# Eleven idle matmuls between the last transposes of q' and the first k^T v of batch 0

## The chip, the cores and the metric

The kernel runs on one core of a Trainium2 chip. The metric is the device time of one execution in microseconds (us). A core has five engines with queues of their own: TensorE (PE, with its weight loads as PEld), VectorE (DVE), ScalarE (ACT), GpSimd (POOL) and SyncE (SP). They wait for each other by semaphores. Each engine takes its instructions in the order in which the program lists them.

## The reference

Linear attention with cosine weights, and a feed-forward layer on its output. The shapes are 8 batches, 8 heads, 576 positions and a head dimension of 64; the layer has d_model 512 and d_ff 2048, on 4608 rows.

```python
def phi(x, c, s):                       # c = cos(pi/2 * pos/S), s = sin(pi/2 * pos/S)
    r = np.maximum(x, 0.0)
    return np.concatenate([r * c, r * s], axis=-1)
q_p, k_p = phi(q, c, s), phi(k, c, s)   # 64 -> 128 columns
kv  = np.einsum('bhsf,bhsd->bhfd', k_p, v)
z   = np.sum(k_p, axis=2)
num = np.einsum('bhsf,bhfd->bhsd', q_p, kv)
den = np.einsum('bhsf,bhf->bhs', q_p, z)[..., None] + 1e-06
x   = (num / den), as rows of (batch, position) by 512
h = x @ w_in
out = (h * sigmoid(1.702 * h)) @ w_out
```

## The kernel before

All of it runs in bf16 with sums in f32. The rows of x are cut into nine blocks of 512. A block's first layer is `mm1` (line 281: four matmuls of 128x512 for each of 16 slices of d_ff, then a gelu on ACT, line 286), its second is `mm2` (line 321: 16 matmuls of 128x512 for each of four row tiles). In the main loop from line 476 the attention of batch i + 1 is laid between the matmuls of block i, at steps written out by hand. The order on every engine is the order of the program text: the schedule is manual.

Before that loop stands a start of its own for batch 0, lines 356 to 473; the change lies in it. It runs as follows.

- `warmup(12)` (line 422) issues twelve matmuls of 128x512 on a tile of zeros, `warm`; nothing reads their result. They stand in PE's queue while q of batch 0 is on its way.
- For four quarters (n, p) of q, the half of the heads n and the pair of row chunks p, `prep_q0` makes q' = relu(q) times cosine and sine (line 207 on DVE, line 205 on ACT), and `turn_q0` turns it: eight transposes on PE (line 364) into one bank of the tile `mm`, and one copy on ACT to `qT` (line 365). After each quarter but the last, `warmup(2)` adds two idle matmuls.
- `prep(0, "k", ...)` makes k' the same way, twelve calls: for the first half of the heads chunks 0 to 5, and then for the second half. All cosines are on DVE; of the sines, those of chunks 3 to 5 are on ACT (line 205), the others on DVE.
- `kv0` (line 373) is k^T v and the sum of k' in one: for each head six matmuls, one for each chunk, with 128 columns (v and a column of ones, stepped over). `kv_lo` has heads 0 to 3, `kv_hi` heads 4 to 7 in two calls; ACT casts each part to `kvs` (line 375).
- `num0` (line 382) makes numerators and denominators for half of the heads and two row chunks, eight matmuls with 65 columns. `den0` and `product0` divide on DVE (lines 392 to 401), `turn_x0` turns the result on PE (line 409) and ACT copies it to `xT` (line 411).
- `mm1_first` (line 417) makes the first four slices of the first layer for block 0 in parts, as the pieces of `xT` come.

PSUM tiles come from two rings: `mm`, four buffers of one bank each, and `at`, two buffers of two banks each. A tile's first writer waits until the readers of the buffer's last tile are done. In the start `mm` serves the four `turn_q0`, then `kv_lo`, `kv_hi` and the four accumulators of `mm1_first`, in this order. The idle matmuls of `warmup` take an `at` tile.

k of batch 0 is loaded by POOL's queue in two halves and v in three parts (line 86), behind q, which SP's queue loads (line 120).

Of the kernel before, what the change touches and what calls it, by code (L numbers as in the profile page):

```python
# [21 lines left out]
def kernel(  # L22
# [9 lines left out]
    nc = tc.nc  # L32
# [21 lines left out]
    def rows(c):  # L54
        return 128 if c < 4 else 64

    def wide(b, n):
        return b < 2 and n != "q"

    def krows(b, c):  # L60
        return 96 if b < 2 else rows(c)

    warm = const.tile([128, TB], BF16)
    nc.vector.memset(warm, 0.0)

    def mm_tile():
        return ps.tile([128, TB], F32, name="mm", bufs=4)

    def at_tile():
        return ps.tile([128, 2, 512], F32, name="at", bufs=2)  # L70

    def warmup(n):
        wps = at_tile()
        for _ in range(n):
            nc.tensor.matmul(wps[:, 0], warm[:, 0:128], warm, start=True, stop=True)


    state = {b: {} for b in range(B)}
# [103 lines left out]
    def part(b, n, c, h0, h1):  # L182
        if wide(b, n):
            return state[b][n][:96, 0:48 * D].rearrange("p (h c d) -> p c h d", c=6, d=D)[:, c, h0:h1]
        if c == 4:
            return state[b][n, 4].rearrange("p (h d) -> p h d", d=D)[:, h0:h1]
        return state[b][n][:, 0:32 * D].rearrange("p (h c d) -> p c h d", c=4, d=D)[:, c, h0:h1]
# [7 lines left out]
    def qn_slot(b, c):  # L195

        return state[b]["qn4"] if b < 2 and c == 4 else state[b]["qn"][:rows(c), c]

    def prep(b, n, c, h0=0, h1=H, on=(nc.vector, nc.vector)):
        r = rows(c) if n == "q" else krows(b, c)  # L200
        for cs, w in enumerate((cos6, sin6) if wide(b, n) else (cosw, sinw)):
            o = qn_slot(b, c) if n == "q" else kp[:r, c]
            oc, i, wc = o[:, h0:h1, cs * D:cs * D + D], part(b, n, c, h0, h1), w[:r, c:c + 1]
            if on[cs] is nc.scalar:
                nc.scalar.activation(oc, i, AF.Relu, scale=wc)  # L205
            else:
                nc.vector.tensor_scalar(oc, i, 0.0, wc, op0=MAX, op1=MUL)  # L207
# [159 lines left out]
    def kv0(kv, h0, h1):  # L367

        v3 = s0["v"][:96].rearrange("p (j d) -> p j d", d=D)
        for h in range(h0, h1):  # L370
            for c in range(6):
                j = h * 6 + c
                nc.tensor.matmul(kv[:, ts(h % 4, 128)].rearrange("p (j d) -> p j d", j=2), kp[:96, c, h, :],  # L373
                                 v3[:, j:49:48 - j, :], start=(c == 0), stop=(c == 5))
        nc.scalar.copy(s0["kvs"][:, h0 // 4, h0 % 4:h0 % 4 + h1 - h0, 0:D + 1],
                       kv.rearrange("p (h e) -> p h e", e=128)[:, h0 % 4:h0 % 4 + h1 - h0, 0:D + 1])
# [43 lines left out]
    AC, VE = nc.scalar, nc.vector  # L420
    kvs_new(0)
    warmup(12)

    def prep_q0(n, p, on=(VE, VE)):
# [5 lines left out]
    for n, p in ((0, 0), (0, 1), (1, 0), (1, 1)):  # L430
        if n:
            prep_q0(n, p)
        turn_q0(n, p, AC.copy)
        if (n, p) != (1, 1):
            warmup(2)
    for n in range(2):
        for c in range(6):
            prep(0, "k", c, 4 * n, 4 * n + 4, on=(VE, AC if c > 2 else VE))
    kv_lo, kv_hi = mm_tile(), mm_tile()
    kv0(kv_lo, 0, 4)  # L440
    kv0(kv_hi, 4, 6)
# [122 lines left out]
```

## Time and profile before

| | |
|---|---|
| median of 4 runs | 300.36 us |
| the runs | 298.69, 300.30, 300.42, 302.07 us |
| the profiled execution | 298.91 us |
| its span, first to last instruction | 296.9 us |
| PE busy in the span | 284.2 us (96%) |
| mean granted clock of PE | 0.991 |
| `warmup` (line 75) matmuls | 18, 379/492/634 ns (least, median, most) |
| k^T v (line 373) matmuls | 48, of 219 ns in the median |

The profile is of one execution. Times in it are in us from the first instruction, and "idle before" a group is the time that its engine stood still ahead of it, with what ended the wait. Matmuls are pipelined: one of 219 ns is followed by the next after a quarter of that, so the distance between starts tells more than the duration. The granted clock is that of PE, as a share of the full one.

### The profile page before, as it was taken

What the parts mean: (1) busy time and instruction counts of PE and PEld (TensorE: products, weight loads), DVE (VectorE), ACT (ScalarE), POOL (GpSimd) and SP (SyncE); (2) the same over time, 40 slices, a digit from 0 to 9 for tenths busy, and PEclk for the clock granted to TensorE, in tenths of its full rate; (3) what the DMA queues carried; (4) which work ended last, traced back from release to release, by engine and by line L of the source; (5) the groups of instructions that cost most, each with busy time, mean ns of one, the idle gap of its engine ahead of it and who ended that gap; (6) DMA issues with size and microseconds to landing.
All of it is one profiled execution on the core that took longest, in us unless ns stands there. A gap on an engine that the chain in (4) does not pass through costs nothing.

```text
span 296.9 us, 5089 instructions
## 1 busy us (share of the span) xinstructions
PE 284.2 (96%) x1940; PEld 146.9 (49%) x1974; DVE 105.7 (36%) x357; ACT 126.0 (42%) x215; POOL 94.8 (32%) x117
## 2 busy tenths in 40 slices
PE   8778999999999999999999999999999999999994
PEld 3575456545444554455445544554455444444443
DVE  5751454683490158115811482148214200000000
ACT  6836623663127412651175116511751166127411
POOL 8542330540259025800690159004401200120021
PEclk9979999999999999999999999999999999999998
DMA  8999999599999977995799879965902510011033
GB/s 195 186 204 199 203 198 191 154 127 173 155 208 170 185 121 137 183 193 100 137 179 174 124 138 194 186 104 116 194 3 60 121 42 1 35 71 38 0 71 71
DMA packets 87303, 39.65 MB, mean 134 GB/s; under 512 B 57136, under 2 KB 85040, under 8 KB 87280
## 3 DMA queue, kind: packets, MB, share of 16 engines
q0 software_dynamic: 40848, 27.01, 58.6%
q1 hardware_dynamic: 46272, 12.20, 24.4%
q8 instruction: 15, 0.25, 0.3%
q10 hardware_dynamic: 160, 0.13, 0.2%
q14 instruction: 8, 0.07, 0.1%
HBM read 36.70 MB, written 9.44 MB: 155 GB/s over the span
## 4 chain that ended last, share of the span: by engine, by line
PE 87%; DMA 5%; DVE 3%; ACT 3%; issue 1%; ACTq 0%; DVEq 0%
PE mm L281 39%; PE mm L321 37%; DMA qT<-qn 4%; PE at L265 3%; PE at L244 3%; PE mm L417 2%; DMA q<-in_q_dram 1%; DVE qn L207 1%; PE mm L345 1%; ACT g L286 1%; PE mm L373 1%; DVE xb L273 1%; ACT qT L226 1%; ACT kp L205 0%; PE mm L364 0%
## 5 line engine op out<-in xcount | busy, mean ns | idle before, releaser
L321 PE MATMUL mm<-w_out_sb,g 128*128 128x512 bf16 x543 | 126.4, 379 | 0.6
L281 PE MATMUL mm<-xT,w_in_sb 128*128 128x512 bf16 x547 | 122.7, 377 | 0.9
L333 POOL DMA_DIRECT2D out_dram<-ysb x54 | 50.6, 941 | 174.4 <-ACT ysb L331 172.9
L286 ACT ACTIVATE g<-mm 128x512 bf16<-128x512 f32 x144 | 85.6, 598 | 45.9 <-PE mm L281 44.9
L281 PEld LDWEIGHTS <-w_in_sb 128*128 128x128 bf16 x564 | 54.4, 98 | 64.1 <-issue 0.2
L321 PEld LDWEIGHTS <-g 128*128 128x128 bf16 x560 | 52.1, 98 | 57.0
L331 ACT COPY ysb<-mm 128x512 f32<-128x512 f32 x34 | 19.9, 585 | 98.3 <-PE mm L321 94.9
L248 DVE CAST kvs<-at 128x260 bf16<-128x260 f32 x14 | 5.4, 426 | 60.5 <-PE at L244 60.5
L273 DVE TENSOR_TENSOR xb<-at,inv 128x512 bf16<-128x512 f32 (+1 forms) x36 | 24.8, 689 | 1.2
L271 DVE TENSOR_SCALAR den<-at 128x8 f32<-128x8 f32 (+1 forms) x36 | 5.9, 164 | 44.4 <-PE at L265 44.4
L350 DVE COPY ysb<-mm 128x256 f32<-128x256 f32 x1 | 0.4, 424 | 59.4 <-PE mm L345 59.4
L265 PEld LDWEIGHTS <-qT 128*128 128x128 bf16 x272 | 12.9, 98 | 8.8 <-DMA qT<-qn 0.9
L207 DVE TENSOR_SCALAR qn<-q,cosw 128x512 bf16<-128x512 bf16 (+1 forms) x36 | 12.7, 356 | 11.4 <-DMA q<-in_q_dram 11.4
L265 PE MATMUL at<-kvs,qT 128*128 128x65 bf16 x272 | 14.2, 194 | 1.0 <-DMA qT<-qn 0.4
L207 DVE TENSOR_SCALAR qn<-q,sinw 128x512 bf16<-128x512 bf16 (+1 forms) x34 | 13.0, 381 | 0.0
L86 POOL DMA_DIRECT2D v<-in_v_dram x10 | 9.3, 943 | 5.3 <-DMA w_in_sb<-in_moe_w_in_dram 2.7
L244 PEld LDWEIGHTS <-kp 128*128 128x128 bf16 (+1 forms) x288 | 9.6, 97 | 1.6
L244 PE MATMUL at<-vt,kp 128*128 128x65 bf16 (+1 forms) x288 | 9.8, 193 | 0.0
L86 POOL DMA_DIRECT2D k<-in_k_dram x9 | 7.8, 865 | 4.1 <-DMA q<-in_q_dram 3.3
L207 DVE TENSOR_SCALAR kp<-k,cosw 128x512 bf16<-128x512 bf16 x24 | 8.3, 348 | 0.0
L207 DVE TENSOR_SCALAR kp<-k,sinw 128x512 bf16<-128x512 bf16 x24 | 8.1, 336 | 0.0
L272 DVE RECIPROCAL inv<-den 128x8 f32<-128x8 f32 (+1 forms) x36 | 7.2, 201 | 1.2
(75 smaller groups left out, 136.2 us busy)
## 6 DMA issues: line engine op xcount, KB each, us to landing
out_dram<-ysb POOLq DMA_DIRECT2D x38, 128.0 KB, 2.9
out_dram<-ysb POOLq DMA_DIRECT2D x16, 256.0 KB, 2.7
q<-in_q_dram POOLq DMA_DIRECT2D x7, 512.0 KB, 9.2
k<-in_k_dram POOLq DMA_DIRECT2D x6, 512.0 KB, 10.7
v<-in_v_dram POOLq DMA_DIRECT2D x6, 512.0 KB, 12.2
w_out_sb<-in_moe_w_out_dram POOLq DMA_DIRECT2D x4, 512.0 KB, 18.3
w_in_sb<-in_moe_w_in_dram POOLq DMA_DIRECT2D x3, 512.0 KB, 12.1
q<-in_q_dram SPq DMA_DIRECT2D x2, 512.0 KB, 4.3
```

What stands on the lines that cost most here:

```text
L86: on.dma_start(out=state[b][n][:np_, t * D * h0:t * D * h1].rearrange("p (h e) -> p h e", h=h1 - h0), in_=SRC[n][b, h0:h1, 0:np_ * t, :].r ...
L207: nc.vector.tensor_scalar(oc, i, 0.0, wc, op0=MAX, op1=MUL)
L244: nc.tensor.matmul(kv[:, ds(h % 4 * (D + 1), D + 1)], kp[:r, c, h, :], vt[:r, c, h, 0:D + 1], start=(c == 0), stop=(c == last))
L265: nc.tensor.matmul(nm[:, h // 4, ds(h % 4 * (D + 1), D + 1)], q_slot(b, c)[:, h, :], state[b]["kvs"][:, h // 4, h % 4, 0:D + 1], start=Tru ...
L272: nc.vector.reciprocal(inv[:r], den[:r])
L273: nc.vector.tensor_tensor(state[b]["xb"][:r, c].rearrange("p (n h) d -> p n h d", n=2), nm4[:, :, :, 0:D], inv[:r].unsqueeze(3).to_broadca ...
L281: nc.tensor.matmul(hps[:, c0:c1], w_in_sb[:, kc, ds(fc * 128, 128)], xT[:, kc, ds(i * TB + c0, c1 - c0)], start=(kc == 0), stop=(kc == KC ...
L286: nc.scalar.activation(g, hps, AF.Gelu_apprx_sigmoid)
L321: nc.tensor.matmul(yps, gT[fc][:, ds(t * 128, 128)], w_out_sb[:, fc, :], start=(fc == 0), stop=(fc == FC - 1))
L331: nc.scalar.copy(ysb, cur[t])
L333: nc.gpsimd.dma_start(out=out[row:row + (n - 1) * step + 1:step, :], in_=ysb[p0:p0 + n, :])
L417: nc.tensor.matmul(first[fc][:, c0:c1], w_in_sb[:, kc, ts(fc, 128)], xT[:, kc, c0:c1], start=(kc == 0), stop=(kc == KC - 1))
```

## The change

One call of `warmup` is added, between the making of k' and `kv0`, so on PE it stands behind the last eight transposes of q' and ahead of the first matmul of k^T v. It issues eleven matmuls of 128x512 on the tile of zeros. They write a tile of their own from the ring `mm`, so that the tiles taken after it each move on by one buffer in this ring. For that, `warmup` gets a second argument, the tile to write to; without it, it takes an `at` tile as before.

```diff
-    def warmup(n):
-        wps = at_tile()
+    def warmup(n, wps=None):
+        wps = at_tile()[:, 0] if wps is None else wps
         for _ in range(n):
-            nc.tensor.matmul(wps[:, 0], warm[:, 0:128], warm, start=True, stop=True)
+            nc.tensor.matmul(wps, warm[:, 0:128], warm, start=True, stop=True)
...
     for n in range(2):
         for c in range(6):
             prep(0, "k", c, 4 * n, 4 * n + 4, on=(VE, AC if c > 2 else VE))
+    warmup(11, mm_tile())
     kv_lo, kv_hi = mm_tile(), mm_tile()
     kv0(kv_lo, 0, 4)
     kv0(kv_hi, 4, 6)
```

## The prediction

> **What bounds the kernel now.** I read the page first (shares, slices, clock), then PE's waits, the chain over the first 26 us, PE's instructions around the change, and last load and clock in stretches of one length. The page, busy time of PE and two rows of the 40 slices:
>
> ```profile
> PE 284.2 (96%) x1940; PEld 146.9 (49%) x1974; DVE 105.7 (36%) x357; ACT 126.0 (42%) x215; POOL 94.8 (32%) x117
> ...
> PE   8778999999999999999999999999999999999994
> ...
> PEclk9979999999999999999999999999999999999998
> ```
>
> PE bounds the kernel. It stands still mainly in the first four slices (7.42 us each), and in the third its granted clock is not full. Its waits over the run, longest first:
>
> ```profile
> PE mm L373 <- DMA v<-in_v_dram: 1.7, 1, 1.7
> PE at L409 <- DVE xb L401: 1.4, 1, 1.4
> ```
>
> The first is the place of the change. The chain there (start, us, what):
>
> ```profile
> 9.27 0.63 PE mm L364 x8
> 9.90 0.02 issue
> 9.93 0.02 ACT qT L365
> 9.95 0.89 issue
> 10.84 1.31 ACT kp L205 x3
> 12.15 0.05 issue
> 12.20 1.92 PE mm L373 x31
> ```
>
> k^T v (L373) does not follow from PE's work. ACT first evicts the turned q', then makes the sine half of k' for chunks 3 to 5, and the sixth matmul starts at 12.20, when ACT has the third. The first five ran earlier, as PE's own list of instructions shows (start, us, line, tiles, count):
>
> ```profile
> 8.68 0.59 PE L75 MATMUL at<-warm 128*128 128x512 bf16 x2
> 9.11 0.78 PE L364 MATMUL mm<-ident,qn 128*128 128x128 bf16 x8
> 11.59 2.51 PE L373 MATMUL mm<-v,kp 96*128 96x128 bf16 x36 [1.70 <-DMA v<-in_v_dram]
> ```
>
> The clock is seen in stretches of 3.41 us, set where its record changes (stretch, us, PE busy with instructions, the same of PEld, DVE, ACT and POOL, clock, DMA):
>
> ```profile
> 8.43:11.84 3.41, 1.71 (x22) 1.11 (x20) 3.41 (x18) 3.19 (x6) 1.57 (x3) 1.00 1.29 198
> 11.84:15.25 3.41, 3.17 (x57) 2.93 (x55) 1.75 (x8) 2.14 (x6) 2.93 (x4) 1.00 1.17 184
> 15.25:18.66 3.41, 1.58 (x30) 1.28 (x28) 1.82 (x8) 1.40 (x4) 0.89 (x2) 1.00 1.24 207
> 18.67:22.07 3.40, 3.40 (x39) 3.40 (x37) 1.40 (x5) 0.65 (x2) 1.64 (x3) 0.50 1.39 199
> ```
>
> The clock is half in one stretch only, 18.67 to 22.07, right after a stretch of low load. The stretch with the hole that the change fills has low load too, and cost no clock in this execution.
>
> **The change part by part.** *The added matmuls.* The last transpose takes 0.219, so it starts at 9.11 + 0.78 - 0.22 = 9.67; the next instruction can start 0.06 later, at 9.73 (after the group before it: 8.62 to 8.68). Two warm matmuls fill 8.68 to 9.11, 0.215 each; eleven fill 2.37 and end at 12.10. Of these, 9.73 to 11.59 is a hole, free. Then five k^T v matmuls that ran from 11.59 on now run from 12.10: 5 x 0.056 = 0.28 (31 in 1.92 with the drain of the last), and the sixth starts at 12.38 instead of 12.20: **+0.18**. Behind it on PE lie the rest of k^T v, then the numerators (L382); for k^T v waits ACT's cast of kvs (13.46), for the numerators DVE's denominator (14.39). ACT is done with k' at 13.34, so it does not hide the delay, and from 12.20 to 25.4 the chain runs without slack. Behind that PE's waits are under 0.5 us together, on work that PE's own progress released. So the 0.18 reaches the end.
> Bounds: had k' been ready when v landed, all of 11.59 to 12.10 would be exposed, 0.5, and 0.6 with a wake-up; were ACT 0.2 later, nothing. I take 0.18, what these rows give.
>
> *The bank.* The idle matmuls write the mm bank that the first turned q' left; ACT's copy of it ended before 8.69 (two copies from 6.71 in 1.98), so they wait for nothing. All later mm tiles move one bank on: k^T v takes the banks of the second and third copies (done by 10.94 at the latest), the first of the four accumulators the fourth's bank, long free at 18.0. Cost nothing, covered by at least 1 us each; without cover, one copy of about 1 us. The changed signature of the helper costs nothing. No DMA, no queue of SP or POOL, no wait on ACT or DVE is touched.
>
> *The clock.* In the profiled execution the sum is 298.91 + 0.18 = 299.1 (298.91 is its own time: span 296.9 and 2.0 around it). But that execution lies 1.45 below the median of the runs, 300.36, so it is not the typical one, and what can differ is where the clock's stretches fall. I count the columns that PE streamed in a stretch, against 3.41 / 0.215 x 512 = 8120 at full clock. 8.43 to 11.84: 2 x 512, about 12 transposes and 5 k^T v of 128 each = 3200, 0.39; the clock stayed. 15.25 to 18.66: 14 numerators of 65, 6 transposes and 7 first matmuls of 128 = 2570, 0.32; it fell. So it falls from somewhere between 0.32 and 0.39. Now slide the first stretch 0.6 later, 9.03 to 12.44: 8 transposes, some 10 k^T v, the rest of a warm one, 2500, 0.31: below the stretch that fell. At 1.4 later (9.84 to 13.25) 24 k^T v give 3070, 0.38 again. So in about a third of all placements, 0.2 to 1.3 later, the hole should cost a half-clock stretch over k^T v: 3.41/2 = **1.7**. With the eleven matmuls (5632 columns more) every such stretch is over 0.8, so that loss goes. The later hole, before L409, stays; by the same count it costs its 1.7 in the placements that it did, and some others.
> The run times speak for such steps: 298.69, 300.30, 300.42, 302.07 and the profile's 298.91 are about 1.6 apart.
>
> Here stands a rule against the change. The Trainium skill ("TensorE: Matmul & The Clock Gate", "Part 1: The HAM clock gate") has the clock halved after an idle window of about 3.4 us, and its closing table warns of PE idle for more than about 3 us. By it the hole of 1.70 costs no clock, and the change is worth +0.18 on every run: 300.36 + 0.18 = 300.5. Against it stands the stretch at 15.25: its longest hole is 1.44, and the clock was half after it. I go by the row. The same section says that the window runs free of the kernel's start; one execution can't show that, but my slide rests on it.
>
> **The forecast and the rivals.**
> 1. *The forecast.* A typical run loses one half-clock stretch too many to this hole and is rid of it: 300.36 - 1.7 + 0.18 = 298.8 by the stretch, 299.1 by the profiled execution, which had no such loss. I take **299.1**, nearest to a row. Chance 0.50.
> 2. *The hole costs no clock in any run*, and the 1.6 steps come from transfers or from the start. For it: the hole's own stretch kept its clock here. Then 300.5, to 301.0 at the upper bound of the delay. Chance 0.28.
> 3. *Both holes lose their cost.* Where k^T v runs at half clock, all that follows comes 1.7 later, and the second hole can fall into a bad stretch because of that. Then a run that had two loses both: 300.36 - 3.4 + 0.2 = 297.2, and for a median with some runs left at one, 297.4. Against it: the second hole cost its stretch here without the first. Chance 0.14.
> 4. *Slower: the idle matmuls run at half clock themselves.* At the start the warm ones went 0.427 apart (12 from 1.20 to 5.83 with the change of pace in them). If the clock is still or again half at 9.73, eleven take 4.70, k^T v starts at 14.43, and the sixth at 14.71: +2.5, 302.9. It decides from a start of 12.10 on: each 0.1 of pace adds 1.1. Against it: the stretches before 9.73 are loaded (PE 3.02 busy in 5.01 to 8.42). Chance 0.08.
>
> **How the numbers follow.** Likeliest: 299.1. The range takes in cases 1 and 2 with the delay's upper bound (301.0) and reaches case 3's 297.4 below; case 4 and the edges are left out. About 1% (3 us) is what a measurement of this kernel can tell from no change. Faster by more than that (under 297.36) needs all of case 3 and a little more: 0.07. Slower (over 303.36) needs case 4 and k^T v slow besides: 0.03. All else, 0.90, is within.
>
> **What the changed profile would show.** Eleven L75 matmuls of 0.379 from about 9.73, 0.215 apart; L373 from 12.10 with no wait on v's DMA; its sixth some 0.2 later than before; ACT's cast of kvs at about 13.64. The stretch with the hole over 0.8 in columns and full clock after it, in every execution; a half-clock stretch, if any, only after the hole before L409. Wrong would make it: a half clock just after 12 us all the same, L373 later than 12.4, or runs that still lie in steps up to 302.

## The result, and the profile after

| | before | changed |
|---|---|---|
| median | 300.58 us (63 runs) | 299.86 us (44 runs) |
| range | 297.55 to 304.13 | 297.27 to 303.37 |
| ratio to before | | 0.9976, 95% interval 0.9958 to 0.9994 |
| profiled execution | 298.91 us | 301.41 us |

The ratio compares, for each kernel, the mean of the runs within 1.5% of its fastest: 299.47 us (37 of 44 runs) against 300.19 (47 of 63). The changed kernel is 0.7 us faster, clear of its interval. The forecast was 1.26 below the median of four runs, 300.36; from the 300.58 of 63 runs its 299.1 is 1.5 away, and the measured gain is about half of that. The profiled execution of the changed kernel, 301.41, lies above its median and that of before below; so the two profiles tell where time lies, not how much the change is worth. The page of the changed kernel, busy row of PE and two rows of the slices:

```profile
PE 286.7 (96%) x1950; PEld 147.1 (49%) x1985; DVE 106.1 (35%) x357; ACT 125.7 (42%) x215; POOL 97.3 (32%) x117
...
PE   8978999999799999999999999999999999999994
...
PEclk9999999999989999999999999999999999999999
```

The third slice now has its full clock. Slice 11 has an idle part and slice 12 a lowered clock, which the kernel before had not. The waits of PE in the changed kernel name the idle part:

```profile
PE at L265 <- DMA qT<-qn: 2.2, 1, 2.2
PE at L409 <- DVE xb L401: 1.4, 1, 1.4
...
PE mm L373 <- DMA v<-in_v_dram: 0.2, 1, 0.2
```

The hole ahead of k^T v has shrunk from 1.7 to 0.2. At the top stands a wait of the numerators of batch 2 (L265) for the transposes of their q. Before it was 0.42; now it is 2.2. The group of eight matmuls that waits (start, us, and the wait in brackets), in the profile of before and then of the changed kernel:

```profile
79.65 0.43 PE L265 MATMUL at<-kvs,qT 128*128 128x65 bf16 x8 [0.42 <-DMA qT<-qn]
```

```profile
80.52 0.43 PE L265 MATMUL at<-kvs,qT 128*128 128x65 bf16 x8 [2.20 <-DMA qT<-qn]
```

PE's instructions around the change, in the changed kernel:

```profile
8.93 0.70 PE L364 MATMUL mm<-ident,qn 128*128 128x128 bf16 x8
9.46 2.54 PE L75 MATMUL mm<-warm 128*128 128x512 bf16 x10
12.23 2.27 PE L373 MATMUL mm<-v,kp 96*128 96x128 bf16 x36 [0.23 <-DMA v<-in_v_dram]
```

One of the eleven is missing from the trace: its page has eleven weight loads more than before (1985 and 1974) but only ten matmuls more (1950 and 1940). They run at the full-clock distance, but k^T v starts at 12.23 and not behind them: it waits 0.23 for v. The chain says the same:

```profile
3.17 8.92 DMA v<-in_v_dram
12.09 0.14 issue
12.23 2.28 PE mm L373 x36
```

v landed at 12.09 in this execution and by 11.59 in that of before. The idle matmuls cost nothing here. The same stretches of 3.41 us as before, set by this execution's clock record (the last two lie at the new wait):

```profile
9.72:13.12 3.40, 3.12 (x25) 1.72 (x25) 3.40 (x16) 3.35 (x8) 1.90 (x3) 1.00 1.24 182
13.13:16.52 3.39, 2.99 (x57) 2.72 (x54) 1.18 (x5) 0.92 (x3) 2.54 (x5) 1.00 1.24 206
16.54:19.94 3.40, 1.86 (x34) 1.74 (x33) 2.22 (x8) 1.50 (x4) 0.59 (x1) 1.00 1.35 199
77.97:81.38 3.41, 1.21 (x13) 0.56 (x12) 0.36 (x2) 0.59 (x1) 1.04 (x2) 1.00 1.46 165
81.39:84.79 3.40, 3.40 (x16) 1.50 (x15) 1.13 (x4) 0.00 (x0) 0.00 (x0) 0.50 0.79 209
```

The clock holds over the start. The wait of 2.2 leaves PE busy for 1.21 of the stretch that ends at 81.38, and the next one runs at half clock. So one wait costs this execution 2.2 and then, by an estimate from the half-clock stretch of 3.41, up to 1.7 more.

### The profile page after: what moved, and what is told of

It is laid out like the page before. It is cut to its first block, busy times and chain, and to the rows that moved or that the text cites. A ratio compares the mean times of both kernels' runs of the same rounds, so it can differ in the third digit from the quotient of the medians.

```text
span 299.4 us, 5110 instructions
## 1 busy us (share of the span) xinstructions
PE 286.7 (96%) x1950; PEld 147.1 (49%) x1985; DVE 106.1 (35%) x357; ACT 125.7 (42%) x215; POOL 97.3 (32%) x117
## 4 chain that ended last, share of the span: by engine, by line
PE 86%; DMA 7%; ACT 2%; DVE 2%; issue 1%; POOL 1%; ACTq 0%; POOLq 0%; DVEq 0%
PE mm L281 38%; PE mm L321 37%; DMA qT<-qn 4%; PE at L265 3%; DMA v<-in_v_dram 3%; PE at L244 3%; PE mm L417 1%; PE mm L345 1%; PE mm L373 1%; ACT g L286 1%; DVE xb L273 1%; ACT qT L226 1%; ACT xT L411 1%; POOL k L86 0%; PE at L225 0%
## 5 line engine op out<-in xcount | busy, mean ns | idle before, releaser
L321 PE MATMUL mm<-w_out_sb,g 128*128 128x512 bf16 x543 | 127.9, 382 | 0.6
L265 PEld LDWEIGHTS <-qT 128*128 128x128 bf16 x272 | 13.2, 99 | 10.9 <-DMA qT<-qn 2.7
L265 PE MATMUL at<-kvs,qT 128*128 128x65 bf16 x272 | 14.5, 195 | 2.7 <-DMA qT<-qn 2.2
L86 POOL DMA_DIRECT2D v<-in_v_dram x10 | 8.3, 833 | 2.8 <-DMA w_in_sb<-in_moe_w_in_dram 2.8
L95 POOL DMA_DIRECT2D kt<-in_k_dram x6 | 8.1, 1356 | 2.0 <-DMA k<-in_k_dram 2.0
L75 PE MATMUL at<-warm 128*128 128x512 bf16 x18 | 7.0, 546 | 1.2 <-DVE eps L151 1.2
```

The lines of the kernel that those rows point to most:

```text
L75: nc.tensor.matmul(wps, warm[:, 0:128], warm, start=True, stop=True)
L86: on.dma_start(out=state[b][n][:np_, t * D * h0:t * D * h1].rearrange("p (h e) -> p h e", h=h1 - h0), in_=SRC[n][b, h0:h1, 0:np_ * t, :].r ...
L95: on.dma_start(out=t.rearrange("p (h d) -> p h d", h=H), in_=SRC[n][b, :, 512:576, :].rearrange("h p d -> p h d"))
L265: nc.tensor.matmul(nm[:, h // 4, ds(h % 4 * (D + 1), D + 1)], q_slot(b, c)[:, h, :], state[b]["kvs"][:, h // 4, h % 4, 0:D + 1], start=Tru ...
L321: nc.tensor.matmul(yps, gT[fc][:, ds(t * 128, 128)], w_out_sb[:, fc, :], start=(fc == 0), stop=(fc == FC - 1))
```

## The experiments

Three theories were tried. *Theory 1*, the prediction's: the hole ahead of k^T v lowers the clock in part of the executions, and the change stops that. *Theory 2*: so it does, but the wait for the transposes near 80 us takes back part of the gain. *Theory 3*: the hole costs no clock.

Besides its time, each timed run has its mean granted clock, and this is the best evidence for the clock, since a profile shows only one placement of the stretches. A half-clock stretch of 3.41 us takes 3.41/2/297 = 0.0057 off the mean. (A tail of half clock at the very end takes off a little too and costs nothing: 0.002 in the profile of a_late_fill2, which has no other half-clock stretch behind its first 4.13 us.) By that measure a run under 0.988 has about two stretches or more ahead of the tail; those at 0.976 have about four. In the names, b_ is the kernel before with an edit and a_ the changed one:

| kernel | runs | under 0.988 | mean clock | median us | ratio to before, 95% |
|---|---|---|---|---|---|
| before (beside b_late, a_late, a_late_fill2, a_20) | 44 | 22 | 0.9856 | 300.68 | |
| changed | 44 | 0 | 0.9952 | 299.86 | 0.9976 (0.9958 to 0.9994) |
| b_late | 22 | 14 | 0.9846 | 299.75 | 0.9972 (0.9947 to 0.9997) |
| a_late | 10 | 0 | 0.9961 | 297.93 | 0.9919 (0.9886 to 0.9952) |
| a_3_late | 6 | 0 | 0.9962 | 298.36 | 0.9914 (0.9881 to 0.9946) |
| b_late_fill2 | 13 | 2 | 0.9926 | 298.51 | 0.9921 (0.9896 to 0.9947) |
| a_late_fill2 | 11 | 0 | 0.9991 | 297.55 | 0.9909 (0.9880 to 0.9939) |
| a_8_late_fill2 | 5 | 0 | 0.9996 | 297.04 | 0.9882 (0.9852 to 0.9912) |
| a_20 | 14 | 0 | 0.9964 | 301.48 | 1.0018 (0.9981 to 1.0054) |
| a_20_late | 14 | 0 | 0.9949 | 300.60 | 1.0000 (0.9970 to 1.0030) |
| a_ld12 | 11 | 0 | 0.9951 | 299.35 | 0.9975 (0.9940 to 1.0009) |
| b_ld20 | 20 | 13 | 0.9863 | 303.12 | 1.0061 (1.0030 to 1.0093) |
| a_ld20 | 22 | 0 | 0.9959 | 300.78 | 1.0013 (0.9988 to 1.0038) |

The runs fall into four series, each with runs of before beside it. These differ (medians 300.58 to 301.50), so kernels of different series are compared by their ratios. Under 0.988 lie 22 of 44, 10 of 23 and 24 of 49 runs of before in the three series of the experiments.

**The wait near 80 taken away, without and with the change.** The numerators of batch 2 for row chunks 3 and 4 feed block 3 of the first layer, so they can come later. This was put into the kernel before (b_late) and into the changed one (a_late):

```diff
-            k0, k1, ks = (11, 24, (25, 26, 27, 28)) if i == 0 else (0, 12, (17, 19, 21, 23, 25))
+            k0, k1, ks = (11, 24, (25, 26, 27, 28)) if i == 0 else (0, 12, (17, 19, 21, 27, 29) if i == 1 else (17, 19, 21, 23, 25))
```

> The kernel before, with the numerators of batch 2 for its row chunks 3 and 4 moved from steps 23 and 25 of block 1 to steps 27 and 29, so that PE comes to them 3.4 us after the transposes of q that they wait for. Theory 1 (the hole before k^T v costs half-clock stretches, and little is lost later): the wait at 80 us was 0.4, so 0.4 below before, ratio 0.998 to 0.999. Theory 2 (a wait of PE for the transposes of q of batch 2 near 80 us, which land by the load of the DMA engines and not by PE, takes 0.4 to 2.2 us and can cost a half-clock stretch of 1.7 after it): 1 to 2 us below before, ratio 0.993 to 0.997, and no wait for qT over 0.2 near 80.

> The change, with the same later numerators. Theory 1: 0.7 us below before from the change and 0.4 more, ratio 0.996. Theory 2 (what the change gains early is taken by the wait near 80): without that wait the gain is whole, so it is 1 to 1.5 below the kernel before with the later numerators, and 2.5 to 3.5 below before, ratio 0.988 to 0.992. Theory 3 (the hole costs no clock at all, the change is only 0.2 us of matmuls): 0 to 0.2 above the kernel before with the later numerators.

b_late has ratio 0.9972 and a_late 0.9919, and neither profile has a wait for qT of any length that is listed. Between the two the change is worth 0.9919/0.9972 = 0.9947, with the half-widths put together 0.991 to 0.999: 1.6 us. Theory 3 falls, by the time and by the clock: 14 of 22 runs of b_late lie under 0.988 and none of a_late, as 22 of 44 of before and none of the changed kernel. b_late gains 0.8, between what theories 1 and 2 expected; a_late lies where theory 2 had it. The change gains more without the wait than with it (0.53% against 0.24%), as theory 2 said, but these two intervals overlap. The two kernels ran in one series, so their runs can also be set against each other directly: the means are 299.78 and 297.96, 1.8 apart, with a 95% interval of 1.2 to 2.5 if the runs are independent. That excludes 0.7 but just meets the upper end of the 0.7's own interval, 0.2 to 1.3.

**Twenty idle matmuls.** Nine more, 1.94 us, with the wait near 80 (a_20) and without (a_20_late):

```diff
-    warmup(11, mm_tile())
+    warmup(20, mm_tile())
```

> The change with 20 idle matmuls in place of 11, nine more of 0.215 us = 1.9 us later k^T v. If all that comes later at the start reaches the end: 1.9 above the changed kernel, ratio to before 1.004. Theory 2 (PE meets a transfer near 80 us that doesn't come later with it): part of it is taken up there, 0.5 to 1.4 above the changed kernel, ratio 1.000 to 1.002, and the wait for qT near 80 is shorter than the 2.2 of the changed kernel's profile.

> Twenty idle matmuls in place of eleven, with the later numerators, so without the wait near 80. If what comes later at the start then reaches the end whole: 1.94 us above the changed kernel with the later numerators (297.9), 299.9, ratio to before 0.998. With the wait in place nine more cost 1.3. If part is taken up somewhere else: 1.3 here too, 299.2.

With the wait the nine cost 1.0018/0.9976, 0.42% or 1.3 us; without it 1.0000/0.9919, 0.82% or 2.4, somewhat more than the 1.94 of a delay that passes whole. The first figure is in theory 2's range. Both have an uncertainty of over a microsecond, so this agrees with theory 2 and doesn't show it. In the profile of a_20 no wait of PE's matmuls for qT is listed; the weight load of chunk 3 still waits 0.57 for it, and the matmuls start at 80.25, 0.6 later than before.

**The loads of batch 3 moved.** The transposes of q run while POOL's queue loads batch 3. To see whether these share what they need:

```diff
-                at(1, load_all, b + 1)
+                at(12 if i == 1 else 1, load_all, b + 1)
```

> The change, with the numerators where they were, and the loads of batch 3 issued at step 12 of block 1 in place of step 1, so about 10 us later, behind most of the transposes of q of batch 2. If PE's wait near 80 is for transposes that share the DMA engines with these loads: the transposes land 2 us or more earlier, the wait near 80 goes, and the time is 1 to 2 below the changed kernel, like that with the later numerators (ratio to before 0.992 to 0.995). If the transposes take their 11 us of themselves: the wait stays at 0.4 to 2.2 and the time is that of the changed kernel, or longer where batch 3 comes late.

This moved nothing. The loads were issued from 58.04 on, as in the kernel before (57.93): they follow at once on the store ahead of them, so nothing that stands between the two places on POOL's queue held them. The kernel is the changed one in effect, and has its ratio again, 0.9975 after 0.9976. So its profile is a second execution of the change, and a different one. It lost a stretch at the start (17.81 to 21.22 at half clock) and came to the first numerators of batch 2 with `qT` at 73.24, where the profile after came at 72.21 and that of before at 73.13. Its wait for `qT` is short:

```profile
77.96 0.43 PE L265 MATMUL at<-kvs,qT 128*128 128x65 bf16 x8 [0.60 <-DMA qT<-qn]
```

It ended 2.2 before the profile after (299.17 against 301.41). The PE that came 1.0 earlier paid 2.2 and a half-clock stretch at the wait, more than it had gained. These are single executions, not averages.

The next pair puts the loads behind two stores that do wait, for results that PE has at 76 us:

```diff
-                at(1, load_all, b + 1)
+                at(20 if i == 1 else 1, load_all, b + 1)
```

> The change, with the loads of batch 3 put behind the first two stores of block 1 on POOL's queue, which wait for PE's results until 76 us, so that the loads start after the transposes of q of batch 2 have run. If these loads share the DMA engines with the transposes and so set when they land: the transposes' landing falls from 11 us to under 8, no wait for qT over 0.2 near 80, and the time is 1 to 2 us below the changed kernel, ratio to before 0.991 to 0.995. If the transposes take their time without the loads: landing of 10 to 12, the wait stays, ratio 0.997 to 0.998.

> The kernel before with the same later loads of batch 3. If the wait near 80 is what took up part of the change's gain: the difference between this and the changed kernel with the later loads is 1.3 to 1.8 us, as with the later numerators (0.53% of the time), and this kernel is 0.5 to 1 us below before. If it was not: the difference is 0.7, as between the kernels on record.

The transfers issued from 55 to 85 us, of the changed kernel and then of a_ld20 (tiles, queue, count, KB, median us to landing):

```profile
q<-in_q_dram POOLq DMA_DIRECT2D x1, 512.0 KB, 10.1
qT<-qn SPq DMA_TRANSPOSE x5, 11.3
xT<-xb SPq DMA_TRANSPOSE x5, 5.8
```

```profile
q<-in_q_dram POOLq DMA_DIRECT2D x1, 512.0 KB, 8.3
xT<-xb SPq DMA_TRANSPOSE x6, 5.9
qT<-qn SPq DMA_TRANSPOSE x5, 3.4
```

Without the loads beside them the transposes of q land in 3.4 in place of 11.3, and the wait for them is gone. So the loads of batch 3 set that wait. The time did not fall as expected; the loads now lie on the transposes of x, and PE waits there:

```profile
PE mm L281 <- DMA xT<-xb: 2.0, 2, 1.0
```

The kernel before lost 0.6% in the same way (1.4 of that wait), where 0.5 to 1 us less was expected. Between the two the change is worth 1.0013/1.0061 = 0.9952 (0.991 to 0.999), 1.4 us, close to the 1.6 of the late pair: with the wait for qT out of the way by either means, the gain is about twice the 0.7. Again each interval of the ratios alone reaches to 0.7. Set against each other directly, in their one series and without a run of 307.16, they are 2.1 apart, 1.4 to 2.8.

The profile of b_ld20 shows what the prediction had only counted, a placement in which the first hole costs the clock. Stretches by its clock record:

```profile
9.18:12.59 3.41, 1.49 (x17) 0.90 (x16) 3.41 (x19) 3.15 (x6) 1.47 (x2) 1.00 1.27 196
12.60:16.00 3.40, 3.40 (x39) 3.40 (x37) 0.43 (x3) 1.52 (x5) 2.61 (x4) 0.50 1.24 205
16.02:19.42 3.40, 1.67 (x30) 1.43 (x28) 2.50 (x9) 0.93 (x3) 1.29 (x2) 1.00 1.26 207
19.43:22.82 3.39, 3.39 (x39) 3.39 (x39) 0.90 (x2) 1.01 (x3) 1.30 (x2) 0.50 1.37 199
```

The stretches lie 0.75 later than in the profile of before. The one with the hole has PE busy for 1.49, and k^T v follows at half clock; then the second hole, the wait of 1.4 for DVE ahead of L409, does it again.

```profile
12.42 3.36 PE L373 MATMUL mm<-v,kp 96*128 96x128 bf16 x31 [0.17 <-ACT kp L205]
```

31 matmuls of k^T v take 3.36 in place of 1.92. The numerators of batch 1's tail start at 71.92, against 70.55 in a_ld20, whose profile has one half-clock stretch instead of two: 1.37 for a stretch.

**Less filling, and filling elsewhere.** If the load of a stretch counts and not the standing still, a few matmuls will do (a_3_late), and the second hole can be filled too (a_late_fill2) or alone (b_late_fill2); eight in the first end before v lands (a_8_late_fill2). The `warmup` ahead of k^T v has three matmuls in a_3_late, eleven in a_late_fill2, eight in a_8_late_fill2 and is left out of b_late_fill2; the second `warmup`, of seven, is in all but a_3_late. All have the later numerators.

```diff
-    warmup(11, mm_tile())
+    warmup(3, mm_tile())
...
+    warmup(7, mm_tile())
     turn_x0(nb0, 1, 0, (0, 1))
```

> Three idle matmuls in place of eleven in the hole before k^T v, with the later numerators of batch 2. They end at about 10.4, so over 1 us of the hole stays open, and k^T v is not delayed. Count theory (the clock is halved after a stretch with less than about a third of the columns): 1536 columns more lift the worst stretch from 0.29 to 0.48, so no half-clock stretch after this hole, clocks as with eleven (no run under 0.988), and 0 to 0.2 below the kernel with eleven. Rival (what counts is how long PE stands still): a hole of 1.2 us still halves the clock in part of the runs, a third of the runs under 0.988, and the time is about halfway back to the kernel without the matmuls, 0.5 to 0.9 us longer.

> The change with the later numerators, and seven more idle matmuls (1.5 us) in the second hole, ahead of the turn of the first x pieces that wait for DVE. Theory of the count (a stretch of 3.41 us with less than about a third of the columns halves the next): no half-clock stretch before 60 us in any placement, mean clock 1.0 apart from the very end, and 0.5 us (a third of 1.7) below the kernel without the second filling on the mean. Rival (the clock falls by something other than the count): the half-clock stretch after 18 us comes as often as before, and the time is the same or up to 0.1 longer.

> No idle matmuls in the first hole, seven in the second (ahead of the turn that waits for DVE), with the later numerators. If the first hole is what cost the many half-clock stretches: runs under 0.988 still make up a third or more, and the time is 0.3 to 0.5 below the kernel before with the later numerators, still 1 us above the one with both holes filled. If the second hole was the cause of most and the first only shifted it: no run under 0.988, and time like that with both filled. A profile of it that falls into a bad placement shows the half clock from 11 to 13 us on over k^T v.

> Both holes filled and the later numerators, with eight idle matmuls in the first hole in place of eleven, so that they end at about 11.45, before v has landed: k^T v starts when its data are there, 0 to 0.2 earlier, and the clock is full throughout. Time 0 to 0.2 below the kernel with eleven and both holes filled, ratio to before 0.990. Rival (the added matmuls of themselves cost their delay of 0.18 and more): 0.3 or more below.

Three matmuls hold the clock as eleven do: no run of six under 0.988, ratio 0.9914 beside 0.9919. In its profile the hole still has 0.67 of waiting for v, and 0.17 twice for ACT. The stretch with the hole (8.54 to 11.96) has PE busy for 2.43 and full clock after it. This speaks for the count, but six runs are few, and the hole that was left is shorter than the 1.2 that was to test the rival. With both holes filled the start had no half-clock stretch, in the profiles of both kernels and by the mean clocks of 0.9991 and 0.9996; the fastest of them, a_8_late_fill2, is at 0.9882 of before, 3.5 us, the best version here. That it takes eight and not eleven in the first hole is within the uncertainty, and so is what a_late_fill2 gains on a_late: 0.3 (-0.4 to 0.9) by their means, where 0.5 was expected.

b_late_fill2 was expected to keep a third of its runs under 0.988, and 0.3 to 0.5 us of gain on b_late. It has 2 of 13, and 0.9921, the gain of a_late. So the many stretches do not come from the first hole alone, as I had it: either filling takes away most runs with two or more. What the first hole costs by itself, with the second filled and the wait near 80 gone, is the difference between b_late_fill2 and a_8_late_fill2, which ran in one series: 0.9882/0.9921 = 0.9961, 1.2 us (0.6 to 1.8 by their runs directly, without one of 301.79), and 0.9996 - 0.9926 = 0.0070 of the mean clock, 1.2 stretches. Ten of the 13 runs of b_late_fill2 lie at 0.994 or under and none of the five. The profile of b_late_fill2 is of one of its two bad runs, and the bad stretch is the first hole's. Stretches by its clock record:

```profile
8.75:12.15 3.40, 1.14 (x12) 0.52 (x9) 3.37 (x16) 3.23 (x6) 1.45 (x2) 1.00 1.28 196
12.17:15.56 3.39, 3.34 (x32) 3.37 (x33) 1.05 (x5) 1.54 (x4) 2.63 (x4) 0.50 1.24 205
15.58:18.98 3.40, 3.15 (x38) 3.02 (x37) 1.15 (x4) 0.54 (x2) 1.28 (x3) 0.50 1.24 207
18.99:22.39 3.40, 3.40 (x14) 1.48 (x13) 1.34 (x6) 0.58 (x1) 1.58 (x3) 0.50 1.39 200
```

Three stretches in a row run at half clock, 10.2 us, although PE is busy nearly throughout (3.34, 3.15 and 3.40). The seven matmuls of the second hole run at half clock here and take twice their time:

```profile
19.08 3.19 PE L75 MATMUL mm<-warm 128*128 128x512 bf16 x7
22.06 0.42 PE L409 MATMUL at<-ident,xb 128*128 128x128 bf16 x2
```

The turn that they precede comes at 22.06. So case 4 of the prediction, idle matmuls at half clock, occurs at another place. The execution took 301.8, against 297 for the runs of this kernel at 0.998 and 0.999.

## Why the prediction was off

*The direction and the mechanism* (case 1) held. The hole lowers the clock in part of the executions, and the eleven matmuls end that: 22 of 44 runs under 0.988 become none of 44. Case 2 (no clock lost, by the rule of an idle stretch of about 3 us that the prediction quotes from the Trainium skill, "TensorE: Matmul & The Clock Gate", "Part 1: The HAM clock gate", and its closing table) is refuted by the same numbers and by the profile of b_ld20, where PE stood for 1.5 and the clock fell. The slide of the stretches is borne out too: in the 13 profiles the clock first turns full between 4.13 (a_late_fill2) and 6.29 us (changed) after the first instruction, and the two bad profiles lie 0.32 and 0.75 later than that of before, inside the 0.2 to 1.3 of the prediction. Case 4 is refuted by the profile after: 0.215 apart, k^T v at 12.23.

*The step that failed* is "Behind that PE's waits are under 0.5 us together, on work that PE's own progress released. So the 0.18 reaches the end", which I let stand for the gain as well. The reading was wrong: the waits behind 25.4 are 0.4 for `qT` and 0.3 for ACT's copy, 0.7 together, and the first was read as PE's own work and so as fixed. It is a transfer's landing, lengthened from 3.4 to 11 by loads beside it, and a PE that is early waits for it: 2.2 in the profile after, with a half-clock stretch behind. The forecast of -1.26 measured -0.7 with that wait in place, and -1.6 and -1.4 with it taken out in two ways (-1.8 and -2.1 by the runs directly). That the wait took part of the gain fits both pairs, both kernels with twenty and the two profiles of the change; by the ratios no pair's interval excludes 0.7, and by the runs directly both do, so it is likely and not certain. Why the landing moves is open: the transposes were issued 0.9 earlier in the profile after than before (58.02 and 58.94) and were there 0.9 later, and I have no run that says why.

*The terms of the sum.* A typical run was to lose one stretch of 1.7 to the first hole. That did not follow from the prediction's own count, which gave the loss to a third of the placements, 0.6 on the mean. The hole costs more often than that: by itself, with what follows from it, 1.2 stretches and 1.2 us on the mean (b_late_fill2 and a_8_late_fill2). So the 1.7 was too large by about 0.5, and that the one stretch of the forecast is close to these 1.2 is luck. Where the second hole is open too, more is lost. By the mean clock the change takes off 0.9952 - 0.9856 = 0.0096, and 0.0115 in the late pair: 1.7 and 2.0 stretches on the mean, from the two holes together as case 3 had it. But a stretch is worth less than 1.7. In a_late, runs at clock 1.0 took 297.2 and at 0.994 298.7, 1.5 a stretch; in b_late, runs at 0.994 took 298.4 and at 0.976 301.1, 2.7 for 3.1 stretches, 0.9 each. Why it is so little I have only an argument for: half clock costs where PE is what the chain waits for, and between the numerators and the turns the chain waits for DVE and ACT (16.03 to 17.61 and 17.96 to 18.35 in the profile of before). More stretches than forecast, at a lower price each, gave a gain near the forecast in the late pair: errors that offset each other, and so luck.

*The delay of 0.18* was not seen: v landed 0.5 later in the profile after than in that of before, which covered it, and three matmuls, which end before v lands, did no better than eleven, within the uncertainty of 0.4%.

*The spread.* I took steps of 1.6 in five run times for single stretches of one hole. The steps are there, but mixed: clock stretches of 0.9 to 1.5, and the wait near 80. The changed kernel still spreads from 297.3 to 303.4, and without the wait, in a_late, from 297.1 to 298.8: the steps up to 302 that were to be gone are mostly those of the wait.

## What to carry to other kernels

A gain at the start can be lost again at the next transfer that does not come earlier with it: look for the small wait on a DMA downstream, ask what sets its landing, and reckon that it may grow (here from 0.4 to 2.2). Idle matmuls in a short hole paid here, where stretches of low load lay between dense ones; three did about as well as eleven. A loss that falls on a third of the placements belongs in the sum with a third of its size. Where the state of the clock differs from run to run, one profile is a sample, and the mean clock of many timed runs says more than it.

## What the runs showed of the hardware that was not expected

The half clock did not always end after one stretch, though PE was busy all through it. From 12.17 to 15.56 in b_late_fill2 PE was busy for 3.34 of 3.39 at half clock, on k^T v with 96 rows, and the next stretch was still at half; after 18.67 to 22.07 in the profile of before, matmuls with 128 rows, it was full again. In b_ld20, 12.60 to 16.00, k^T v too, it was full after one. What decides between these is not shown.

At full clock, in the stretches shown here, the clock fell after PE had been busy for 1.14, 1.21, 1.49, 1.58 and 1.67 of 3.41, and held after 1.71 (before) and 1.86 (after). The count of columns from the prediction, made for the first 100 us of all 13 profiles, orders them as well: ten stretches stand ahead of a fall, with 0.23 to 0.37 of the columns of a full one, and all that held had 0.39 or more. At half clock the count fails, since the stretch from 12.17 in b_late_fill2 and that from 12.60 in b_ld20 both had 0.50. Weighted with the rows in use (96 of 128 for k^T v) they have 0.38 and 0.39, and the stretch from 15.58 in b_late_fill2, after which the clock stayed at half, has 0.37. But by this weight one that held, 8.43 to 11.84 in the profile of before, also has 0.37. A single transpose at the edge of a stretch makes 0.016, so the weighted count may be the measure for both clocks; no run here tests it, or tells it from the busy time at full clock.

Transposes by DMA land three times later beside loads: 11.3 against 3.4.
